# Product 6 of a fused spectral filter and feed-forward kernel: its second half's partial sums in the "kept" buffers, its rows of x in "fs" and "fx", and the loads of the last tile issued during the tile before

## The chip, the cores and the metric

The kernel runs on one core of one Trainium2 chip. The metric is the device time of one execution in microseconds, lower is better. Each core has a TensorE (PE) for matmuls, a VectorE (DVE), a ScalarE (ACT), a GpSimd (POOL) and a SyncE (SP), whose work here is to issue transfers. SyncE and ScalarE each have a queue of transfers of their own, and every engine works through its instructions in the order in which the program gives them.

## The reference

```
x = A_x                                  # 2048 x 1024
xn = layernorm(x)
X = rfft2(xn) * (w_r + 1j * w_i)
s = irfft2(X)                            # 2048 x 1024
h = silu(xn @ w1)                        # 1024 -> 3584
g = silu(h @ w2)                         # 3584 -> 1024
return x + s * g
```

All inputs and the output are float32, with 2048 rows in all.

## The kernel before

The program is one stream of Python that writes the instructions of all engines in an order made by hand. It has three long parts: `xn @ w1` (the matmuls of line 456) with the forward transform beside it, then `h @ w2` (lines 534 to 536) with the filter and the inverse transform beside it, and a short end. Products of float32 numbers are made from three float16 matmuls (high by high, high by low, low by high).

**Seven products instead of eight.** `h @ w2` is computed over groups of 128 rows and halves of 512 columns. Instead of the eight block products of a 2 by 2 block matrix product, seven products of sums and differences of blocks are formed (line 32 names the left factors, line 33 the blocks of w2), and the outputs are put together from them by additions. The products are numbered m = 0 to 6, and each has eight tiles j = 0 to 7: g = j // 4 says which pair of row classes (c = 2g and 2g + 1), p = j % 4 which 128 rows of these. The loop at line 1545 runs over `seq`, all (m, j) with m outermost, so the last eight tiles are those of product 6, and this document calls them tile 0 to tile 7. "First half" is tiles 0 to 3 (g = 0), "second half" tiles 4 to 7.

**One tile.** `mm2` (line 530) does half of a tile's contraction in 21 matmuls of 512 columns (k = 0 and k = 1). The hidden activations `ht` come from memory by `load_h` (line 513), two tiles ahead, on ScalarE's queue. The last tile is cut into three pieces of 256, 128 and 128 columns (line 1552), so that its arithmetic after the matmuls can begin earlier.

**What product 6 does with its result.** It completes two finals per tile. `load_parts` (line 524) reads two partial sums of 128 x 512 back from memory, `pl` from `pd[2, j]` and `pd[0, j]`, on SyncE's queue. When the tile's matmuls are done, `evac` (lines 600 to 602) subtracts the product from the one and adds it to the other on VectorE (lines 601 and 602). `final` (line 620) applies silu on ScalarE (line 622), in place. `finish_out` (line 613) multiplies by the spectral part `s` (line 615) and adds x (line 616) on VectorE, again in place, and puts the store to the output (line 618) on SyncE's queue, or, for the two last pieces of one of the halves, on ScalarE's.

**Rows.** The 128 x 512 pieces of `s` (`fs`) and of x (`fx`) that `finish_out` needs are "rows": `rows_for` (line 540) loads them on SyncE's queue, `ahead_rows` (line 554) calls it early. In the first half of product 6 both are loaded, so a tile has four of them; in the second half `s` is still in its buffer (`resident`, line 1336; the profile calls it `rows`), so only two pieces of x are loaded.

**Stages.** Work after the matmuls is spread over the following tiles by `settle` (line 1421): between the halves of tile j + 1 come first `finish_out` of tile j - 1 and then lines 601 and 602 of tile j; at the end of tile j + 1 come the two activations of tile j. Then `load_parts` and `ahead_rows` of tile j + 1 are written (lines 1568 and 1569), and after them `tick` (line 175) puts out the stores of tile j - 1. So SyncE's queue holds, tile after tile: two partial sums, the rows, two stores of the tile two before. For the last tile `load_parts` and `ahead_rows` stand ahead of its first piece (lines 1550 and 1551).

**Buffers.** `tile_of` (line 203) takes a buffer from a group named by a tag. The buffers of a tag are used in turn: a new user waits until the last reader or writer of that buffer is done. The tags that matter:

| tag | buffers of 128 x 512 | used by |
|---|---|---|
| kept | 8 | running sums of products 0 to 5 (one for each j), then the rows of product 6 |
| pt | 6 | partial sums that are written (products 1, 3, 5) or read back (4, 6) |
| fs | 3 | rows of `s` for finals of other products |
| fx | 2 | rows of x for finals of other products |

A partial sum that is read back is overwritten by lines 601, 602, 622, 615 and 616 and then stored from the same buffer, so its buffer becomes free when that store has landed. A row's buffer is free when VectorE has read it.

Of the kernel before, what the change touches and what calls it, by code (L numbers as in the profile page):

```python
# [10 lines left out]
F32 = mybir.dt.float32  # L11
# [116 lines left out]
def spectral_ffn(ctx, tc, x, w_r, w_i, w1, w2, ca, kc, ci, tw, pm, out):  # L128
# [15 lines left out]
    H = {"p": hstack.enter_context(tc.tile_pool(name="hid", bufs=1))}  # L144
    pf = ctx.enter_context(tc.tile_pool(name="pf", bufs=4, space=PSUM))
    pt = ctx.enter_context(tc.tile_pool(name="pt", bufs=2, space=PSUM))
# [28 lines left out]
    def tick():  # L175
        due = []
        for d in deferred:
            d[0] -= 1
            if d[0] <= 0:
                due.append(d)  # L180
        for d in due:
            deferred.remove(d)
            d[1]()
# [7 lines left out]
    def store(tag, n, fn):  # L191

        d = [n, None]

        def run():
            held[tag].remove(d)
            fn()

        d[1] = run
        held.setdefault(tag, []).append(d)  # L200
        deferred.append(d)

    def tile_of(pool, shape, dtype, name, tag, bufs):
        while len(held.get(tag, ())) >= bufs - 1:
            d = held[tag][0]
            deferred.remove(d)
            d[1]()
        return pool.tile(shape, dtype, name=name, tag=tag, bufs=bufs)
# [302 lines left out]
    part, ht = {}, {}  # L511

    def load_h(m, j, k, queue=nc.scalar):
        t_ = fp.tile([128, 7, 2, 128], F16, name=f"ht{m}_{j}_{k}", tag="w1", bufs=7)
        queue.dma_start(t_, hd[PRODUCTS[m], j // 4][:, j % 4, 7 * k:7 * k + 7])
        ht[m, j, k] = t_
# [4 lines left out]
    rows = {}  # L521
    READS = ((), (), (), (), (1, 0), (), (2, 0))

    def load_parts(m, j):
        for k in READS[m]:
            t_ = tile_of(H["p"], [128, 512], F32, f"pl{m}_{j}_{k}", "pt", 6)
            nc.sync.dma_start(t_, pd[k, j])
            part[k, j] = t_

    def mm2(m, j, ps, k, cols=slice(0, 512)):  # L530
        for q in range(7):
            hh, w = ht[m, j, k][:, q], w2t[m, k][:, q, :, cols]
            first, last = (k + q == 0), (k + q == 7)
            nc.tensor.matmul(ps, hh[:, 0], w[:, 0], start=first, stop=False)  # L534
            nc.tensor.matmul(ps, hh[:, 0], w[:, 1], start=False, stop=False)  # L535
            nc.tensor.matmul(ps, hh[:, 1], w[:, 0], start=False, stop=last)  # L536

    kept = {}

    def rows_for(c, p, h, pool, tags):  # L540

        hsl = slice(h * 512, (h + 1) * 512)
        if (c, p) in sstore:
            sstore.pop((c, p))()
        t_ = []
        for name, src, (tag, bufs) in (("fs", sd[c, p], tags[0]), ("fx", xs[4 * c + p], tags[1])):
            if name == "fs" and (c, p) in resident:
                t_.append(resident[c, p][:, hsl])
                continue
            t_.append(tile_of(pool, [128, 512], F32, f"{name}{c}_{p}_{h}", tag, bufs))  # L550
            nc.sync.dma_start(t_[-1], src[:, hsl])
        return t_

    def ahead_rows(m, j):
        g, p = j // 4, j % 4
        tags = (("kept", 8), ("kept", 8)) if m == 6 else (("fs", 3), ("fx", 2))
        for c, h in FINALS[m]:
            if (2 * g + c, p) in stile and (2 * g + c, p, h) not in rows:
                rows[2 * g + c, p, h] = rows_for(2 * g + c, p, h, H["p"], tags)

    def acc(m, j, ps, cols=slice(0, 512)):
        tt = nc.vector.tensor_tensor
        g, p = j // 4, j % 4
        ahead_rows(m, j)

        def fresh(name):
            return tile_of(H["p"], [128, 512], F32, f"{name}_{j}", "pt", 6)

        def keep(k, t_):
            store("pt", 3, lambda: nc.sync.dma_start(pd[k, j], t_))  # L570

        def evac():
            if m == 0:
                kept[j] = H["p"].tile([128, 512], F32, name=f"kept{j}", tag="kept", bufs=8)
                nc.scalar.activation(kept[j], ps, AF.Copy)
            elif m == 1:
                t_ = fresh("c11")
                tt(t_, kept[j], ps, op=OP.subtract)
                keep(0, t_)
            elif m == 2:  # L580
                tt(kept[j], kept[j], ps, op=OP.add)
            elif m == 3:
                t_ = fresh("c21")
                nc.scalar.activation(t_, ps, AF.Copy)
                tt(kept[j], kept[j], ps, op=OP.subtract)
                keep(1, t_)
            elif m == 4:
                t_, u = part.pop((1, j)), part.pop((0, j))
                tt(t_, t_, ps, op=OP.add)
                tt(u, u, ps, op=OP.add)  # L590
                keep(0, u)
                return final(2 * g + 1, p, 0, t_)
            elif m == 5:
                t_ = fresh("c12")
                nc.scalar.activation(t_, ps, AF.Copy)
                tt(kept[j], kept[j], ps, op=OP.add)
                keep(2, t_)
                return final(2 * g + 1, p, 1, kept.pop(j))
            else:
                t_, u = part[2, j][:, cols], part[0, j][:, cols]  # L600
                tt(t_, t_, ps, op=OP.subtract)  # L601
                tt(u, u, ps, op=OP.add)
                a_, b_ = final(2 * g, p, 1, t_, cols), final(2 * g, p, 0, u, cols)

                def both():
                    x_, y_ = a_(), b_()
                    return (lambda: (x_ and x_(), y_ and y_(), None)[2]) if x_ or y_ else None

                return both

        return evac

    def finish_out(tag, c, p, h, o, s_, x_, cols=slice(0, 512)):
        first = h * 512 + cols.start
        nc.vector.scalar_tensor_tensor(o, s_, s_sc, o, op0=OP.mult, op1=OP.mult)
        nc.vector.tensor_tensor(o, o, x_, op=OP.add)
        queue = nc.scalar if cols.start and h else nc.sync
        store(tag, 1, lambda: queue.dma_start(outs[4 * c + p][:, first:first + cols.stop - cols.start], o))

    def final(c, p, h, o, cols=slice(0, 512)):  # L620
        def act():
            nc.scalar.activation(o, o, AF.Silu, scale=c2)  # L622
            tag = "kept" if h and c % 2 else "pt"
            if (c, p) not in stile:
                store(tag, 1, lambda: nc.sync.dma_start(gd[c, p, h], o))
                fins[c, p, h] = True
                return None
            t_ = rows.get((c, p, h)) or rows_for(c, p, h, H["p"], (("fs", 3), ("fx", 2)))
            return lambda: finish_out(tag, c, p, h, o, *(v[:, cols] for v in t_), cols)

        return act
# [778 lines left out]
    with tc.manual_schedule():  # L1410
# [21 lines left out]
        def after(ev):  # L1432
            settle()
            fresh_ev[0] = ev
            tick()
            work()
# [108 lines left out]
        for n, (m, j) in enumerate(seq):  # L1545
            if 0 < n < len(seq) - 2:
                for k in range(n == 1, 2):
                    load_h(*seq[n + 2], k, nc.scalar)
            if n == len(seq) - 1:
                load_parts(m, j)  # L1550
                ahead_rows(m, j)
                for b, cols in enumerate((slice(0, 256), slice(256, 384), slice(384, 512))):
                    ps = pf.tile([128, cols.stop - cols.start], F32, name=f"pb{m}_{j}_{b}", tag="ff")
                    for k in range(2):
                        mm2(m, j, ps, k, cols)
                    for _ in range(4):
                        settle()
                        tick()
                    after(acc(m, j, ps, cols))
                break  # L1560
            ps = pf.tile([128, 512], F32, name=f"pb{m}_{j}", tag="ff")
            for k in range(2):
                while ready2[0] < m * NP + 7 * k + 6:
                    slot(wq)
                mm2(m, j, ps, k)
                if k == 0:
                    settle()
                    load_parts(m, j)
                    ahead_rows(m, j)
                    tick()  # L1570
                    work()
            if j == 7:
                done2[0] = m + 1
            after(acc(m, j, ps))
            if m == 0:
                slot(wq)
# [38 lines left out]
```

## Time and profile before

| what | value |
|---|---|
| median of 3 runs | 1241.05 us |
| lowest and highest of them | 1239.05 and 1243.32 us |
| the profiled execution, whole | 1238.48 us |
| its span, first to last instruction | 1236.6 us |
| PE busy | 1221.4 us |
| DVE busy | 998.6 us |
| ACT busy | 467.3 us |
| POOL busy | 117.3 us |
| moved by DMA | 293.67 MB, mean 237 GB/s |
| TensorE clock granted, mean | 0.998 |

Times inside the profile are microseconds from the start of the span, unless marked as ns. A row of the timeline gives the start, the length, the engine, the line of the kernel, the operation, the buffer written and those read, the shape, and in brackets the idle time before it with what ended it. Rows of transfers are marked SPq or ACTq for the queue; their length is that of the issue, not of the transfer, and several alike are joined (x2). Buffer numbers are left out in the profile, so all partial sums are `pl`; which tile a row belongs to follows from the order. In the chain of waits each step is followed back to what released it, and a transfer's length there runs from its issue to its landing.

### The profile page before, as it was taken

The page shows a single profiled execution, that of the slowest core. Times are in us where ns is not written, and L with a number is a line of the kernel's source. Part 1 is how long each engine was busy: PE and PEld are TensorE (multiplying, and loading weights), DVE is VectorE, ACT ScalarE, POOL GpSimd, SP SyncE. Part 2 cuts the span into 40 slices and gives each one's busy share as a digit, 9 for nine tenths or more (in the row PEclk, how much of TensorE's full clock was granted, in tenths as well). Part 3 has the DMA queues.
Part 4 walks back from the last instruction along what each step waited for, and adds up shares of the span by engine and source line. Part 5 has one row for each costly group of instructions (what it writes and reads, how often), then busy time and mean ns, then how long its engine had stood idle before and what let it go on. Part 6 is the DMA issues. An engine that isn't in the chain of part 4 may idle for free.

```text
span 1236.6 us, 19106 instructions
## 1 busy us (share of the span) xinstructions
PE 1221.4 (99%) x7033; PEld 624.6 (51%) x7033; DVE 998.6 (81%) x1970; ACT 467.3 (38%) x614; POOL 117.3 (9%) x245
## 2 busy tenths in 40 slices
PE   8999999999999999999999999999999999999997
PEld 5545445444544454445445555554455555555544
DVE  7687988899798898886959899985196678798885
ACT  4865344333454565344533222122032222342212
POOL 2330000001000000010001121114111110000000
PEclk9999999999999999999999999999999999999999
DMA  8487476655768898759899999987979999997677
GB/s 251 136 171 186 134 224 204 186 147 166 218 178 237 283 280 242 213 178 272 206 287 223 281 256 200 303 251 238 294 206 275 293 287 320 319 348 292 223 261 231
DMA packets 271102, 293.67 MB, mean 237 GB/s; under 512 B 40096, under 2 KB 198816, under 8 KB 270624
## 3 DMA queue, kind: packets, MB, share of 16 engines
q1 hardware_dynamic: 250992, 233.66, 65.4%
q10 hardware_dynamic: 15984, 51.45, 12.0%
q0 software_dynamic: 4032, 7.34, 3.4%
q8 instruction: 55, 0.90, 0.3%
q14 instruction: 39, 0.32, 0.1%
HBM read 185.95 MB, written 102.25 MB: 233 GB/s over the span
## 4 chain that ended last, share of the span: by engine, by line
PE 87%; DMA 6%; DVE 4%; ACT 1%; issue 1%; SPq 0%; POOL 0%; ACTq 0%; DVEq 0%; POOLq 0%
PE pa L456 45%; PE pb L534 11%; PE pb L536 11%; PE pb L535 11%; DMA out_dram<-pl 2%; PE fx L945 2%; PE id L1285 1%; DMA sd<-s 1%; PE fx L947 1%; PE iu L1195 1%; PE fx L946 1%; ACT xp L700 1%; PE iu L1203 1%; DMA pl<-pd 1%; DMA fs<-sd 1%
## 5 line engine op out<-in xcount | busy, mean ns | idle before, releaser
L456 PE MATMUL pa<-xnT,w 128*128 128x512 f16 x2688 | 585.2, 379 | 1.1 <-ACT w L251 0.7
L456 PEld LDWEIGHTS <-w 128*128 128x128 f16 x2688 | 261.7, 98 | 312.1 <-DVE w L254 1.3
L534 PE MATMUL pb<-w,ht 128*128 128x512 f16 (+2 forms) x812 | 300.6, 372 | 0.0
L535 PE MATMUL pb<-w,ht 128*128 128x512 f16 (+2 forms) x812 | 300.6, 372 | 0.0
L536 PE MATMUL pb<-w,ht 128*128 128x512 f16 (+2 forms) x812 | 300.6, 372 | 0.0
L536 PEld LDWEIGHTS <-ht 128*128 128x128 f16 x812 | 79.3, 98 | 91.2
L534 PEld LDWEIGHTS <-ht 128*128 128x128 f16 x812 | 79.4, 98 | 86.8
L535 PEld LDWEIGHTS <-ht 128*128 128x128 f16 x812 | 79.3, 98 | 86.8
L465 ACT ACTIVATE h<-pa,s 128x512 f32<-128x512 f32 x112 | 75.5, 678 | 120.9 <-PE pa L456 108.9
L251 ACT ACTIVATE w<-jr,sc 128x512 f16<-128x512 f32 x98 | 68.1, 713 | 78.3 <-DMA jr<-in_B_w_dram 39.4
L254 DVE SCALAR_TENSOR_TENSOR hoone<-h,hs,hoone 128x2048 f16<-128x2048 f32 x28 | 65.7, 2345 | 8.9 <-ACT hoone L251 8.9
L254 DVE SCALAR_TENSOR_TENSOR w<-jr,sc,w 128x512 f16<-128x512 f32 x98 | 71.0, 743 | 2.1 <-ACT w L251 2.1
L251 ACT ACTIVATE hoone<-h,hs 128x2048 f16<-128x2048 f32 x28 | 56.0, 1998 | 38.5 <-DVE h L499 25.1
L251 ACT ACTIVATE hosum<-hr,hs 128x1536 f16<-128x1536 f32 x28 | 44.1, 1574 | 65.2 <-DVE hr L495 31.7
L972 ACT ACTIVATE zq<-Z,zs 128x1024 f16<-128x1024 f32 x16 | 18.4, 1149 | 107.6 <-DVE Z L1046 60.8
L254 DVE SCALAR_TENSOR_TENSOR hosum<-hr,hs,hosum 128x1536 f16<-128x1536 f32 x28 | 50.7, 1812 | 3.8 <-ACT hosum L251 3.8
L494 DVE TENSOR_TENSOR hr<-h 128x1024 f32<-128x1024 f32 x28 | 34.2, 1221 | 23.2 <-ACT h L465 23.1
L251 ACT ACTIVATE w<-w1r,rs 128x1024 f16<-128x1024 f32 x28 | 32.0, 1145 | 46.6 <-DVE w L254 31.4
L274 DVE TENSOR_REDUCE m<-w1r 128x1 f32<-128x1024 f32 x28 | 33.8, 1211 | 17.9 <-DMA w1r<-in_B_w_dram 17.9
L622 ACT ACTIVATE pl<-pl,c 128x512 f32<-128x512 f32 (+2 forms) x28 | 17.6, 657 | 72.3 <-DVE pl L601 33.9
L945 PE MATMUL fx<-vq,kq 128*128 128x256 f16 x192 | 43.2, 273 | 0.0
L946 PE MATMUL fx<-vq,kq 128*128 128x128 f16 x192 | 42.1, 219 | 0.0
(219 smaller groups left out, 1526.2 us busy)
## 6 DMA issues: line engine op xcount, KB each, us to landing
w1r<-in_B_w_dram SPq DMA_DIRECT2D x28, 512.0 KB, 6.3
hd_sum<-hosum SPq DMA_DIRECT2D x56, 256.0 KB, 2.9
hd_one<-hoone SPq DMA_DIRECT2D x56, 256.0 KB, 3.6
hd_dif<-hoone SPq DMA_DIRECT2D x56, 256.0 KB, 3.2
w2m<-in_B_w_dram SPq DMA_DIRECT2D x28, 512.0 KB, 5.2
ht<-hd_dif ACTq DMA_DIRECT2D x32, 448.0 KB, 6.0
jr<-in_B_w_dram SPq DMA_DIRECT2D x56, 256.0 KB, 6.8
ht<-hd_sum ACTq DMA_DIRECT2D x32, 448.0 KB, 5.5
```

The lines of the kernel that those rows point to most:

```text
L251: nc.scalar.activation(hi, raw, AF.Copy, scale=scale)
L254: nc.vector.scalar_tensor_tensor(lo, raw, scale, hi, op0=OP.mult, op1=OP.subtract)
L274: nc.vector.tensor_reduce(m1[:, i:i + 1], raw[i], axis=AX.XY, op=OP.max, apply_absolute_value=True)
L456: nc.tensor.matmul(ps, w[:, wh, d], xt[:, xh, d], start=(n == 0), stop=(n == 23))
L465: nc.scalar.activation(hq[:, 2 * (c % 2) + f % 2], ps, AF.Silu, scale=s1[:, f:f + 1])
L494: tt(sums[:, 0:2], hq[:, 0::2], hq[:, 1::2], op=OP.subtract)
L534: nc.tensor.matmul(ps, hh[:, 0], w[:, 0], start=first, stop=False)
L535: nc.tensor.matmul(ps, hh[:, 0], w[:, 1], start=False, stop=False)
L536: nc.tensor.matmul(ps, hh[:, 1], w[:, 0], start=False, stop=last)
L945: nc.tensor.matmul(o, k[:, c, kh, 1], v[:, c, vh], start=(n == 0), stop=False)
L946: nc.tensor.matmul(ps[:, c, 0], k[:, c, kh, 2], v[:, c, vh, 128:256], start=False, stop=False)
L972: nc.scalar.activation(zqs[q][:, 0, :, 16 * j:16 * j + 16], zs_[u], AF.Copy, scale=zs)
```

## The change

Three edits, all of them around product 6:

- The partial sums of tiles 4 to 7 are read into buffers of tag "kept" (`home`), two for each tile, and those of the first half stay in "pt". The tag is handed on to `final` so that the stores are counted under the right tag.
- The rows of x of tiles 4 to 7 go to other tags: for the half of columns h = 1 to "fs", for h = 0 to "fx", and in tile 7 to "pt".
- `load_parts` and `ahead_rows` of tile 7 are called during tile 6, right after those of tile 6, and no longer ahead of tile 7's first piece. `load_parts` passes over partial sums that have been asked for already.

```diff
+    def home(m, j):
+        return ("kept", 8) if m == 6 and j >= 4 else ("pt", 6)
+
     def load_parts(m, j):
         for k in READS[m]:
-            t_ = tile_of(H["p"], [128, 512], F32, f"pl{m}_{j}_{k}", "pt", 6)
+            if (k, j) in part:
+                continue
+            t_ = tile_of(H["p"], [128, 512], F32, f"pl{m}_{j}_{k}", *home(m, j))
             nc.sync.dma_start(t_, pd[k, j])
             part[k, j] = t_
...
     def ahead_rows(m, j):
         g, p = j // 4, j % 4
-        tags = (("kept", 8), ("kept", 8)) if m == 6 else (("fs", 3), ("fx", 2))
         for c, h in FINALS[m]:
+            tags = (("kept", 8), ("kept", 8)) if m == 6 else (("fs", 3), ("fx", 2))
+            if m == 6 and j >= 4:
+                tags = (("kept", 8), ("fs", 3) if h else ("fx", 2) if j < 7 else ("pt", 6))
             if (2 * g + c, p) in stile and (2 * g + c, p, h) not in rows:
...
-                a_, b_ = final(2 * g, p, 1, t_, cols), final(2 * g, p, 0, u, cols)
+                tag = home(m, j)[0]
+                a_, b_ = final(2 * g, p, 1, t_, cols, tag), final(2 * g, p, 0, u, cols, tag)
...
-    def final(c, p, h, o, cols=slice(0, 512)):
+    def final(c, p, h, o, cols=slice(0, 512), tag=None):
+        tag = tag or ("kept" if h and c % 2 else "pt")
+
         def act():
             nc.scalar.activation(o, o, AF.Silu, scale=c2)
-            tag = "kept" if h and c % 2 else "pt"
...
             if n == len(seq) - 1:
-                load_parts(m, j)
-                ahead_rows(m, j)
                 for b, cols in enumerate((slice(0, 256), slice(256, 384), slice(384, 512))):
...
                     load_parts(m, j)
                     ahead_rows(m, j)
+                    if (m, j) == (6, 6):
+                        load_parts(m, 7)
+                        ahead_rows(m, 7)
                     tick()
                     work()
```

## The prediction

> **What bounds the kernel now.** I read the busy time of each engine by stretches first, then the chain of waits that ended last, then the timeline of SyncE's queue, of TensorE and of VectorE over the last 45 us.
>
> Stretches (length, then PE, PEld, DVE, ACT, POOL busy with their counts, TensorE clock, DMA share, GB/s):
>
> ```profile
> 0.00:93.00 93.00, 87.18 (x472) 47.30 (x473) 69.04 (x102) 59.52 (x53) 25.21 (x62) 1.00 0.71 186
> 93.00:1229.08 1136.08, 1134.24 (x6563) 577.33 (x6561) 925.36 (x1854) 406.38 (x558) 92.07 (x183) 1.00 0.82 242
> 1229.08:1236.60 7.52, 0.00 (x0) 0.00 (x0) 4.21 (x15) 1.39 (x4) 0.00 (x0) 0.71 0.45 155
> ```
>
> TensorE is busy for all but 1.84 us of the middle 1136 and all but 5.82 us of the first 93. Then follow 7.52 us in which it does nothing. An edit that touches only the last product's second half can't shorten TensorE's work; it can only shorten this tail, or starve TensorE before it.
>
> What the tail is made of, by the chain of waits (start, length, what):
>
> ```profile
> 1211.00 5.90 DMA out_dram<-pl
> ...
> 1218.77 5.26 DMA out_dram<-pl
> ...
> 1224.41 4.35 DMA fx<-in_A_x_dram
> 1228.86 0.42 DVE pl L616
> ```
>
> These are transfers, not arithmetic. The queue of SyncE says which:
>
> ```profile
> 1199.90 2.00 SPq L527 DMA_DIRECT2D pl<-pd  x2
> ...
> 1208.59 0.89 SPq L527 DMA_DIRECT2D pl<-pd  x2
> ...
> 1216.30 0.94 SPq L527 DMA_DIRECT2D pl<-pd  x2
> ...
> 1218.30 0.85 SPq L618 DMA_DIRECT2D out_dram<-pl  x2
> 1223.43 0.94 SPq L527 DMA_DIRECT2D pl<-pd  x2
> 1224.41 0.90 SPq L551 DMA_DIRECT2D fx<-in_A_x_dram  x2
> ```
>
> The four pl rows are the partial sums of tiles 4, 5, 6 and 7 of product 6. Six "pt" buffers hold three tiles' pairs, so tile 7 needs the pair of tile 4, and that is free only when tile 4's two stores (issued at 1218.30) have landed: the second took 5.26 us to 1224.03. Tile 7's partial sums are thus asked at 1223.43 and its rows of x at 1224.41, when TensorE is already through the first 256 columns of that tile. SyncE's own waits show the pattern (us in total, times, longest):
>
> ```profile
> SPq L527 <- DMA out_dram<-pl: 17.6, 8, 4.8
> ```
>
> Now the end itself, TensorE beside VectorE (start, us, engine, line):
>
> ```profile
> 1219.42 0.38 PE L536 MATMUL pb<-w,ht 128*128 128x512 f16 x1
> ...
> 1224.12 0.27 PE L536 MATMUL pb<-w,ht 128*128 128x256 f16 x1
> ...
> 1228.86 0.22 PE L536 MATMUL pb<-w,ht 128*128 128x128 f16 x1
> ```
>
> ```profile
> 1219.84 0.69 DVE L601 TENSOR_TENSOR pl<-pl,pb 128x512 f32<-128x512 f32 x1 [1.98 <-PE pb L536]
> ...
> 1223.59 0.69 DVE L616 TENSOR_TENSOR pl<-pl,fx 128x512 f32<-128x512 f32 x1
> 1226.16 0.42 DVE L601 TENSOR_TENSOR pl<-pl,pb 128x256 f32<-128x256 f32 x1 [1.88 <-DMA pl<-pd]
> ...
> 1228.86 0.42 DVE L616 TENSOR_TENSOR pl<-pl,fx 128x256 f32<-128x256 f32 x1 [1.22 <-DMA fx<-in_A_x_dram]
> ...
> 1230.06 0.28 DVE L601 TENSOR_TENSOR pl<-pl,pb 128x128 f32<-128x128 f32 x1
> ...
> 1231.99 0.28 DVE L601 TENSOR_TENSOR pl<-pl,pb 128x128 f32<-128x128 f32 x1
> ```
>
> Tile 6 is taken up 0.04 us after its last matmul ends (1219.42 + 0.38 to 1219.84). The first piece of tile 7 is ready at 1224.39 (1224.12 + 0.27) but taken up at 1226.16, and stops again 1.22 us for x. The two last pieces queue behind it on VectorE: the last starts at 1231.99, though TensorE ended at 1229.08 (1228.86 + 0.22). That is 2.91 us of lateness in the tail, and all of it is transfers that were asked late.
>
> **The change part by part.** *Partial sums of tiles 4 to 7 in "kept".* The eight kept buffers hold, in this order, the rows of finals of tiles 0, 1, 2, 3 (four each, in turn). Tiles 4 and 5 now take the four of tile 2, tiles 6 and 7 the four of tile 3. Those are freed by VectorE's finish (lines 615, 616) and by no store:
>
> ```profile
> 1197.06 0.69 DVE L616 TENSOR_TENSOR pl<-pl,fx 128x512 f32<-128x512 f32 x1
> ...
> 1198.45 0.69 DVE L616 TENSOR_TENSOR pl<-pl,fx 128x512 f32<-128x512 f32 x1
> ...
> 1202.70 0.69 DVE L616 TENSOR_TENSOR pl<-pl,fx 128x512 f32<-128x512 f32 x1
> 1203.31 0.68 DVE L601 TENSOR_TENSOR pl<-pl,pb 128x512 f32<-128x512 f32 x1
> 1206.86 0.69 DVE L602 TENSOR_TENSOR pl<-pl,pb 128x512 f32<-128x512 f32 x1 [2.87 <-DMA pl<-pd]
> ...
> 1210.20 0.69 DVE L616 TENSOR_TENSOR pl<-pl,fx 128x512 f32<-128x512 f32 x1
> ```
>
> The first two rows end tile 2's halves at 1197.75 and 1199.14, the third ends tile 3 at 1203.39. So tile 4's pair, asked at 1199.90 and after, can be asked from 1197.75; tile 5's from 1199.14 in place of 1208.59; tile 6's from 1203.39 in place of 1216.30. Counts of instructions, bytes and the order of TensorE, VectorE and ScalarE stay as they are; the same matmuls are issued. What comes sooner first is the idle 2.87 us ahead of line 602 of tile 4: up to 2.87 us of VectorE, worth 0 at the end, since TensorE runs on over it to 1229.08 and tile 6 already waits 1.98 us for TensorE alone.
>
> *Rows of tiles 4 to 7.* With four kept buffers gone to partial sums, x goes to "fs" (three buffers) and "fx" (two), last used by product 5, and once to "pt". Only x is loaded here; the spectral part of these tiles is resident. First waits: the third user of fx (tile 6) and the fourth of fs (tile 7) need tile 4's finish, 1210.89 today (1210.20 + 0.69). This adds a wait that was not there. Queued behind it on SyncE stand tile 7's loads and tile 4's stores; the stores need the same finish anyway.
>
> *Tile 7 asked at tile 6.* Two partial sums, two rows of x: four issues of 0.33 to 0.5 us each, moved ahead of tile 4's two stores. If tile 4's finish stays at its time now, they leave by about 1213.5 (1210.89 plus five issues of up to 0.5); if it comes 2.87 us sooner, by 1210.6. What a landing takes, over all transfers that read or write pl since 1150, and as a median by kind since 1190:
>
> ```profile
> DMA to landing us min/median/max: 1.5/4.5/7.8
> ...
> pl<-pd SPq DMA_DIRECT2D x10, 256.0 KB, 2.7
> fx<-in_A_x_dram SPq DMA_DIRECT2D x10, 256.0 KB, 5.0
> ```
>
> Best case: 1210.6 + 2.7 = 1213.3; worst: 1213.5 + 7.8 = 1221.3. VectorE wants the partial sums at 1224.43 and x some 1.5 us later, so they are there by 3 us at least. I take the late one; it changes nothing. Tile 4's stores go out up to 2 us later behind these, and nothing waits for their buffers any more. Cost of this part if that cover were gone: each us past 1224.43 is a us at the end.
>
> A shared counter matters too. Transfers wait for others that they have nothing to do with:
>
> ```profile
> SPq L570 <- DMA ht<-hd_sum: 5.9, 1, 5.9
> ...
> 1206.84 0.33 ACTq L515 DMA_DIRECT2D ht<-hd_sum  x1
> ...
> 1207.27 1.33 ACT L622 ACTIVATE pl<-pl,c 128x512 f32<-128x512 f32 x2 [6.16 <-DMA out_dram<-pl]
> ```
>
> A store of product 5 waits for hidden activations because the program hands its DMA semaphores round in turn; the load at 1206.84 on ScalarE's queue, for tile 7, delays the activation of tile 4 in the same way. The new order shifts these pairings. Bounds: a gain of up to 3 us for that activation (line 601 ended at 1203.99, it began at 1207.27), or a wait of one landing, at most 7.8 us, on a load that TensorE wants from 1219.64 on and that leaves by 1206.84 now. Both lie in the 9 us and more ahead of tile 7; I take 0.
>
> *Sum.* First piece: taken up at 1224.39 + 0.04 = 1224.43; VectorE is free at 1224.28 (1223.59 + 0.69). It lasts as now, 1226.16 to 1230.06, less the 1.22 for x: 2.68, to 1227.11. Second piece: 1230.06 to 1231.99, 1.93, to 1229.04. Last piece: not before 1229.08 + 0.04 = 1229.12. From its start to the end of the span 4.61 us pass now (1231.99 to 1236.60) and will again. New span 1233.73, **2.87 us less**. The profiled execution took 1238.48, of which 1.88 lie around its span of 1236.60, so 1235.61. The median shown is 1241.05, 2.57 above it (lowest 1239.05): with the same gain **1238.2 us, 0.23% faster**. Within 0.3%, about what a measurement of this kernel can tell from no change, I call it the same.
>
> A rule that speaks against this: SyncE's row above, 17.6 us of waits of the queue itself, shows loads standing still at the head. The Trainium skill, "DMA: Bandwidth & Descriptors", section "Anatomy of one DMA — SWDGE (gpsimd) path", says that the DMA engines never wait on semaphores; the wait is on the issuing sequencer before dispatch. The trace agrees (longest 4.8 us at line 527). By that rule tile 7's loads are early only as long as tile 4's finish is; by the rows it is, and the sum stays.
>
> **Rivals.**
> (1) *The runs lose more in the tail than the profiled one.* The extra 2.57 us of the median must lie in the head (5.82 us idle), the middle (1.84), the tail (7.52) or outside the span (1.88). The tail has the largest part and is a chain of store, load and arithmetic. If half of the extra is there, the gain is 2.87 + 1.29 = 4.2 us: 1236.9; if all, 5.4: 1235.6. I put it at 1236.2. Against it: the head waits for transfers too.
> (2) *The loads crowd each other.* Peaks in the traffic since 1190 (GB/s in 40 slices) reach 414, the mean of the stretch is 243:
>
> ```profile
> GB/s 68 225 337 346 145 309 377 414 380 214 99 280 333 297 385 292 282 264 265 225 394 169 14 159 312 138 274 384 73 187 340 255 370 401 323 148 116 58 56 0
> DMA packets 6391, 11.40 MB, mean 243 GB/s; under 512 B 716, under 2 KB 1484, under 8 KB 6387
> ```
>
> There is room, but if x for tile 7 still came as late against its piece as now while its partial sums came in time, 1.22 stays and the gain is 1.65 or less: 1239.4 to 1241.
> (3) *Slower.* Place: the wait of tile 6's x at the head of SyncE's queue, in front of tile 7's loads. Should tile 4's finish, or the buffer that x needs, come only with the end of tile 6's finish (1224.28), then that x and four loads leave from there, the first x of tile 7 some 1.7 us later than the 1224.41 of today, and the end moves by it: 1242.8 on the median. It decides from a finish of tile 4 after about 1219; it is at 1210.89 now, held up by the 2.87 us of a load that comes sooner, so I see no cause.
> (4) *It doesn't do what it says*: buffers are handed out otherwise, tile 7's partial sums still wait for a store. 1241.05. The rotation seen in the queue (tile 4 behind tile 1's store, tile 7 behind tile 4's) speaks against it.
>
> **How the numbers follow.** Forecast 0.52, (1) 0.30, (2) 0.10, (3) 0.06, (4) 0.02. The line at 0.3% is 3.7 us; the runs shown lie 2 us to either side of their median, so of the forecast's 0.52 I count 0.17 beyond the line and 0.35 within. (1) gives 0.29 and 0.01; (2) and (4) count as the same, 0.12; (3), half beyond its price by the spread of runs, gives 0.05 slower and 0.01 the same. Together faster 0.46, same 0.49, slower 0.05. The range runs from (1) at its full, 1235.4, over the forecast with the spread of a median, to the better half of (2), 1240.8; outside remain (3), (4) and the rest of (2).
>
> **What would show it.** Right: tile 7's partial sums and x issued on SyncE before 1215 and ahead of tile 4's stores; tile 4's line 602 with no wait for a load; line 601 of the first piece released by TensorE at about 1224.4; the last piece starting within 0.2 us of TensorE's end; from TensorE's end to the span's end 4.65 us in place of 7.52. Wrong: a wait of lines 601, 602 or 616 for a load in tile 7; TensorE ending later than 1229.1; a tail over 6 us; or a tail as forecast while the runs change by something else than 3 us, which would put the difference outside the last tile.

## The result, and the profile after

| | kernel before | changed kernel |
|---|---|---|
| median of 11 runs each | 1243.02 us | 1238.23 us |
| lowest to highest | 1239.05 to 1248.68 | 1234.49 to 1241.62 |
| ratio after / before | | 0.9952, 95% interval 0.9934 to 0.9970 |
| profiled execution, whole | 1238.48 | 1235.84 |
| its span | 1236.6 | 1234.1 |

By the ratio the change made the kernel 0.48% faster, which is 6.0 us (3.7 to 8.2 by its interval); the two medians differ by 4.79 us and the two profiled executions by 2.64. First the stretches of the changed kernel, with the cut where its TensorE ends (columns as before: length, PE, PEld, DVE, ACT, POOL, clock, DMA share, GB/s):

```profile
0.00:93.00 93.00, 86.20 (x472) 46.93 (x473) 69.05 (x102) 59.61 (x53) 25.21 (x62) 1.00 0.71 187
93.00:1229.41 1136.41, 1134.54 (x6563) 578.25 (x6560) 928.24 (x1862) 407.32 (x560) 92.14 (x183) 1.00 0.83 243
1229.41:1234.07 4.66, 0.00 (x0) 0.00 (x0) 1.72 (x7) 0.69 (x2) 0.00 (x0) 0.93 0.21 58
```

The tail fell from 7.52 to 4.66 us. TensorE itself ended 0.33 us later than before, and that is what keeps the span from 1233.73. The later end comes from the head, where TensorE is idle for 6.80 us in place of 5.82, long before product 6.

SyncE's queue in the timeline of the changed kernel, where the lines have moved (532 is the load of partial sums, 556 that of rows, 626 the store):

```profile
1198.39 1.61 SPq L532 DMA_DIRECT2D pl<-pd  x2
...
1203.58 1.73 SPq L532 DMA_DIRECT2D pl<-pd  x2
...
1209.71 1.25 SPq L532 DMA_DIRECT2D pl<-pd  x2
1211.52 0.82 SPq L556 DMA_DIRECT2D fx<-in_A_x_dram  x2
1212.51 0.99 SPq L532 DMA_DIRECT2D pl<-pd  x2
1213.80 0.97 SPq L556 DMA_DIRECT2D fx<-in_A_x_dram  x2
1215.09 16.74 SPq L626 DMA_DIRECT2D out_dram<-pl  x10
```

Tiles 4, 5, 6 and 7 now ask at 1198, 1204, 1210 and 1212.5, where it was 1200, 1209, 1216 and 1223. Tile 7's four loads stand ahead of tile 4's stores, 11 us sooner than before. Then VectorE (608 and 609 were 601 and 602, 624 was 616), and TensorE's last matmul of the first piece and its last of all:

```profile
1203.02 0.69 DVE L624 TENSOR_TENSOR pl<-pl,fx 128x512 f32<-128x512 f32 x1
1204.18 0.69 DVE L608 TENSOR_TENSOR pl<-pl,pb 128x512 f32<-128x512 f32 x1 [0.47 <-DMA pl<-pd]
1204.99 0.69 DVE L609 TENSOR_TENSOR pl<-pl,pb 128x512 f32<-128x512 f32 x1
...
1207.83 0.69 DVE L624 TENSOR_TENSOR pl<-pl,fx 128x512 f32<-128x512 f32 x1
...
1224.76 0.42 DVE L608 TENSOR_TENSOR pl<-pl,pb 128x256 f32<-128x256 f32 x1 [0.24 <-PE pb L541]
...
1227.47 0.28 DVE L608 TENSOR_TENSOR pl<-pl,pb 128x128 f32<-128x128 f32 x1
...
1229.44 0.29 DVE L608 TENSOR_TENSOR pl<-pl,pb 128x128 f32<-128x128 f32 x1
```

```profile
1224.44 0.27 PE L541 MATMUL pb<-w,ht 128*128 128x256 f16 x1
...
1229.19 0.22 PE L541 MATMUL pb<-w,ht 128*128 128x128 f16 x1
```

The first piece is released by TensorE and no longer by a load, 0.05 us behind its last matmul; the last piece starts 0.03 us behind TensorE's end. No row of tile 7 waits for a transfer. VectorE's work on the first two pieces (1224.76 to 1229.44) now takes as long as TensorE needs for the other two, so the last piece finds both engines done at nearly the same time.

### The profile page after: what moved, and what is told of

Read it like the earlier page. It is cut to its first block, busy times and chain, and to the rows that moved or that the text cites. A ratio compares the mean times of both kernels' runs of the same rounds, so it can differ in the third digit from the quotient of the medians.

```text
span 1234.1 us, 19097 instructions
## 1 busy us (share of the span) xinstructions
PE 1220.7 (99%) x7033; PEld 625.2 (51%) x7033; DVE 999.0 (81%) x1970; ACT 467.6 (38%) x614; POOL 117.3 (10%) x245
## 4 chain that ended last, share of the span: by engine, by line
PE 75%; DVE 11%; DMA 9%; issue 2%; ACT 1%; SPq 0%; POOL 0%; DVEq 0%; ACTq 0%; POOLq 0%
PE pa L456 45%; PE pb L539 8%; PE pb L541 8%; PE pb L540 8%; DVE Z L1055 2%; DMA wq<-in_A_w_i_dram 2%; DMA sd<-s 2%; PE id L1294 2%; DMA zd<-zq 1%; DMA ht<-hd_sum_d 1%; DVE T L1020 1%; DVE w L254 1%; PE iu L1204 1%; ACT xp L709 1%; PE iu L1212 1%
## 5 line engine op out<-in xcount | busy, mean ns | idle before, releaser
L274 DVE TENSOR_REDUCE m<-w1r 128x1 f32<-128x1024 f32 x28 | 33.8, 1210 | 16.1 <-DMA w1r<-in_B_w_dram 16.1
```

What stands on the lines that cost most here:

```text
L274: nc.vector.tensor_reduce(m1[:, i:i + 1], raw[i], axis=AX.XY, op=OP.max, apply_absolute_value=True)
```

## The experiments

Theory: the gain is the lateness of tile 7's loads and nothing else, so whatever gets them there before 1224 gives it all. Rivals: the place of the request is needed as well as the buffers; the sooner release for tiles 4 to 6 has a part; ordinary executions gain more than the profiled one.

**e1, the new buffers without the earlier request.**

```diff
+                load_parts(m, j)          # tile 7, ahead of its first piece, as before the change
+                ahead_rows(m, j)
...
-                    if (m, j) == (6, 6):
-                        load_parts(m, 7)
-                        ahead_rows(m, 7)
```

> The new buffers stay, tile 7's loads go back to their old place ahead of tile 7's first piece. Theory 1 (the buffers alone free the loads, the earlier place adds nothing): tile 7's partial sums leave SyncE behind tile 4's stores, at about 1214 to 1218 us and not at 1223, land before 1224, line 608 of the first piece is released by TensorE, the tail from TensorE's end is 4.7 us, ratio as that of the whole change, 0.995. Theory 2 (the earlier place is needed): the first piece still waits for a load, tail 6 to 7.5 us, ratio 0.998 to 1.000.

Measured: ratio 0.9960 (0.9942 to 0.9977), median 1235.63 of 7. SyncE's queue, VectorE at the first piece, and the stretch from TensorE's end on:

```profile
1211.19 0.99 SPq L626 DMA_DIRECT2D out_dram<-pl  x2
1212.48 0.98 SPq L532 DMA_DIRECT2D pl<-pd  x2
1213.75 1.01 SPq L556 DMA_DIRECT2D fx<-in_A_x_dram  x2
```

```profile
1223.72 0.42 DVE L608 TENSOR_TENSOR pl<-pl,pb 128x256 f32<-128x256 f32 x1 [0.24 <-PE pb L541]
```

```profile
1228.37:1233.05 4.68, 0.00 (x1) 0.00 (x0) 1.72 (x7) 0.69 (x2) 0.00 (x0) 0.87 0.20 58
```

Theory 1, and the loads are even sooner than I had expected: 1212.48, though they stand behind two stores. The place in the program is not the time: here SyncE issued them 11 us before the matmuls of the first piece were done. With a tail of 4.68 us against 4.66, the third edit of the change is worth nothing beside the other two.

**e2, new buffers for tile 7 alone** (tiles 4 to 6 as before, tile 7 asked during tile 6).

```diff
-        return ("kept", 8) if m == 6 and j >= 4 else ("pt", 6)
+        return ("kept", 8) if m == 6 and j == 7 else ("pt", 6)
...
-            if m == 6 and j >= 4:
-                tags = (("kept", 8), ("fs", 3) if h else ("fx", 2) if j < 7 else ("pt", 6))
+            if m == 6 and j == 7:
+                tags = (("kept", 8), ("fs", 3) if h else ("fx", 2))
```

> Only tile 7 gets new buffers (partial sums in kept, x in fs and fx) and is loaded during tile 6; tiles 4, 5 and 6 stay in pt and kept as before. Theory 1 (only tile 7's lateness is on the path): tile 4's line 609 keeps its wait of some 2.9 us for a load, tile 7's loads leave at 1217 to 1220 us, the tail is 4.7 us and the ratio 0.995. Theory 2 (the sooner release of tiles 4 to 6 is part of the gain): tail between 5 and 7.5 us, ratio 0.997 or above.

Measured: ratio 0.9966 (0.9947 to 0.9984) and a tail of 5.65 us. The tail lies in the range of theory 2; the ratio decides nothing, since its interval reaches into the range of both. As theory 1 had it, line 609 of tile 4 keeps its wait for a load (3.67 us). SyncE's queue, VectorE, and the stretch from TensorE's end on:

```profile
1218.38 0.94 SPq L532 DMA_DIRECT2D pl<-pd  x2
1219.38 0.90 SPq L556 DMA_DIRECT2D fx<-in_A_x_dram  x2
1220.32 0.90 SPq L532 DMA_DIRECT2D pl<-pd  x2
1221.26 0.91 SPq L556 DMA_DIRECT2D fx<-in_A_x_dram  x2
```

```profile
1225.49 0.69 DVE L624 TENSOR_TENSOR pl<-pl,fx 128x512 f32<-128x512 f32 x1 [0.53 <-DMA fx<-in_A_x_dram]
1226.14 0.42 DVE L608 TENSOR_TENSOR pl<-pl,pb 128x256 f32<-128x256 f32 x1
1226.75 0.42 DVE L609 TENSOR_TENSOR pl<-pl,pb 128x256 f32<-128x256 f32 x1 [0.19 <-DMA pl<-pd]
```

```profile
1229.75:1235.40 5.65, 0.00 (x1) 0.00 (x0) 2.65 (x10) 0.80 (x3) 0.00 (x0) 0.84 0.56 193
```

Tile 6's loads (the first row) still wait for tile 3's stores; tile 7's have their buffers but stand behind them. Eight loads go out within 3.8 us, and tile 6's x is so late that VectorE is still finishing tile 6 when the first piece is ready (about 1225.05, 4.70 us ahead of TensorE's end as in the changed kernel), and takes it up at 1226.14. So the theory falls in its narrow form: the release of tiles before tile 7 is part of the gain.

**e8, new buffers for tiles 6 and 7.** Run after the others, to see whether it is tile 6, and not tiles 4 and 5 or the shared semaphores.

```diff
-        return ("kept", 8) if m == 6 and j == 7 else ("pt", 6)
+        return ("kept", 8) if m == 6 and j >= 6 else ("pt", 6)
...
-            if m == 6 and j == 7:
+            if m == 6 and j >= 6:
```

> As e2, but tile 6 too has its partial sums in kept and its x in fs and fx; tiles 4 and 5 stay as before. Theory 1 (e2 kept a tail of 5.6 us because tile 6's loads still waited for tile 3's stores and stood in the queue ahead of tile 7's): tile 6's loads leave before 1216, tile 7's before 1219, line 608 of tile 7's first piece is released by TensorE, tail 4.7 us. Theory 2 (e2's tail came from shared semaphores or from tiles 4 and 5): a wait for a load stays in the first piece, tail 5.2 us or more.

Measured: ratio 0.9971 (0.9953 to 0.9989), and the whole tail is back, in an execution whose TensorE ended at 1230.81. SyncE's queue, VectorE, and the stretch:

```profile
1215.01 1.64 SPq L532 DMA_DIRECT2D pl<-pd  x2
...
1217.91 0.95 SPq L532 DMA_DIRECT2D pl<-pd  x2
```

```profile
1226.15 0.42 DVE L608 TENSOR_TENSOR pl<-pl,pb 128x256 f32<-128x256 f32 x1 [0.24 <-PE pb L541]
```

```profile
1230.81:1235.48 4.67, 0.00 (x0) 0.00 (x0) 1.72 (x7) 0.69 (x2) 0.00 (x0) 0.95 0.21 58
```

Tile 6's loads leave 3.4 us sooner than in e2, in an execution that is 1.1 us later, and that is enough; tile 7's two rows of x left at 1219.10 and after, a little later than the 1219 that I had written. That is theory 1: it is tile 6, and tiles 4 and 5 in the old buffers cost nothing at the end of this trace.

**e5, everything new but asked late.** Tile 7's loads behind its first piece's matmuls.

```diff
                     for _ in range(4):
                         settle()
                         tick()
+                    load_parts(m, j)
+                    ahead_rows(m, j)
                     after(acc(m, j, ps, cols))
```

> All new buffers, but tile 7's partial sums and x are asked only behind its first piece's matmuls, so that SyncE issues them behind the stores of tiles 5 and 6. Theory 1 (when the loads leave is all that counts, not which buffers they use): the partial sums leave at about 1225, land at 1228, x lands at about 1230; the first piece waits for both, the tail is 8 to 9.5 us, longer than the 6.9 and 7.5 of the kernel before; ratio 0.999 to 1.003. Theory 2 (the tail shrank through the buffers themselves, for instance through the stores that are out of the way): tail 4.7 to 6 us, ratio 0.996.

Measured: ratio 1.0000 (0.9981 to 1.0020), median 1242.90. The traced execution ended its matmuls late, at 1237.37; against that end the loads leave 4.5 us ahead, as expected. SyncE's queue and the stretch:

```profile
1231.11 1.72 SPq L626 DMA_DIRECT2D out_dram<-pl  x2
1232.88 0.92 SPq L532 DMA_DIRECT2D pl<-pd  x2
1233.84 0.90 SPq L556 DMA_DIRECT2D fx<-in_A_x_dram  x2
```

```profile
1237.37:1246.71 9.34, 0.00 (x0) 0.00 (x0) 5.46 (x18) 2.40 (x6) 0.00 (x0) 0.74 0.20 61
```

Theory 1: with the same buffers as the changed kernel the tail is 9.34 us, and the whole gain is gone. When the loads leave is what counts. The late end of the matmuls in this execution has another cause, which the last section shows.

**e3, e4, e6, e7, e9, e10: the two kernels again, unchanged.** The ratio was twice what the trace had shown. Copies of both kernels, timed beside each other, show how far their times and their tails spread.

> The changed kernel once more, for a second trace and for the spread. Theory 1 (the gain is the tail, and its size differs from execution to execution with the transfers): tail 4.7 us again, spans differ by 3 us or more because of idle TensorE time elsewhere, at the head. Theory 2 (the tail of the changed kernel is itself longer in some executions): a tail above 5.5 us in this trace or a span that grows with it. Ratio 0.993 to 0.998.

> The kernel before once more, for a second trace and for the spread of spans. Theory 1 (ordinary executions of the kernel before lose more in the tail than the first profiled one): tail from TensorE's end 8.5 to 11 us, TensorE's end within 1 us of 1229, first piece of tile 7 waiting over 3 us for its loads. Theory 2 (they lose it elsewhere): tail 7.5 us, TensorE's end 2 us or more later. Ratio 0.999 to 1.001.

> The changed kernel again, timed in one job with a copy of the kernel before, so that copy stands against copy. Theory 1 (the change is worth its tail, 2.2 to 2.9 us, and what the first comparison showed beyond that is the granted TensorE clock of the single executions): its median lies 2 to 3 us under that of e7, and executions at one granted clock differ by the same. Theory 2 (ordinary executions gain 4 to 6 us): median 4 us or more under that of e7. Tail 4.7 us in its trace by both.

> A copy of the kernel before. Theory 1: ratio to the kernel before 0.998 to 1.001, and where it differs from 1 the granted clocks of the two sets of executions differ too, about 1.2 us for each 0.001. Theory 2: ratio 0.9995 to 1.0005 and clocks alike. Tail 6.9 to 7.6 us in its trace by theory 1, 8.5 us or more by theory 2.

> One more trace of the kernel before, for the spread of its tail, which was 7.5, 6.9 and 9.6 us so far. Theory 1 (the lateness of tile 7's loads hangs on the transfers of each execution): a tail between 6.5 and 10 us, and the later tile 7's second partial sum lands after the first piece's matmuls, the longer. Theory 2 (the tail follows TensorE's end alone): 7 us whenever TensorE ends at 1229.

> As e9, a further trace: by theory 1 a tail between 6.5 and 10 us in step with the landing of tile 7's x, by theory 2 7 us whenever TensorE ends at 1229.

| | median us | ratio (interval) | tail in its trace |
|---|---|---|---|
| e3, after | 1237.81 of 12 | 0.9965 (0.9950 to 0.9980) | 4.66 |
| e6, after | 1237.47 of 12 | 0.9952 (0.9933 to 0.9970) | 4.65 |
| e4, before | 1239.87 of 12 | 0.9992 (0.9977 to 1.0007) | 6.89 |
| e7, before | 1240.73 of 12 | 0.9982 (0.9966 to 0.9998) | 9.62 |
| e9, before | one run, 1240.91 | | 8.90 |
| e10, before | one run, 1239.26 | | 8.63 |
| the kernel before, beside e1 to e4 | 1242.02 of 30 | | |
| the same, beside e5 to e7 | 1243.20 of 29 | | |
| the same, beside e8 to e10 | 1241.45 of 17 | | |

The longest of these tails, the stretch from TensorE's end and VectorE at the first piece of e7:

```profile
1231.78:1241.40 9.62, 0.00 (x1) 0.00 (x0) 5.25 (x17) 1.89 (x5) 0.00 (x0) 0.72 0.58 206
```

```profile
1230.79 0.42 DVE L601 TENSOR_TENSOR pl<-pl,pb 128x256 f32<-128x256 f32 x1 [1.84 <-DMA pl<-pd]
1232.80 0.42 DVE L602 TENSOR_TENSOR pl<-pl,pb 128x256 f32<-128x256 f32 x1 [1.59 <-DMA pl<-pd]
```

In the execution of the prediction the second partial sum cost 0.17 us after the first; here 1.59. The tail of the kernel before is thus 7.52, 6.89, 9.62, 8.90 and 8.63 us in five executions, 8.31 in the mean, while that of the changed kernel is 4.66, 4.66 and 4.65. It doesn't follow TensorE's end: e4 and e10 end their matmuls within 0.2 us of each other, at 1229.04 and 1228.86, with tails of 6.89 and 8.63, which speaks against theory 2 of e9 and e10.

What it follows is how long before TensorE's end tile 7's partial sums are asked for. In e4 and in e7:

```profile
1222.46 0.96 SPq L527 DMA_DIRECT2D pl<-pd  x2
```

```profile
1228.09 1.41 SPq L527 DMA_DIRECT2D pl<-pd  x2
```

That is 6.58 us ahead of the end in e4 and 3.69 in e7; it is 5.65 in the execution of the prediction, 4.74 in e10 and 4.05 in e9. In the order of these leads the tails are 6.89 (e4), 7.52, 8.63 (e10), 8.90 (e9) and 9.62 us (e7): the later the request, the longer the tail, without an exception. This is theory 1 of e9 and e10. Where a program with other buffers asks late, as in e5 (4.49 us ahead), the tail is 9.34 us, some 0.6 us above this row.

The other expectations fared as follows. e4's tail fits neither of its theories, 8.5 to 11 us or a later end of TensorE; the longer tails that its theory 1 wanted are in e7, e9 and e10. For e7 theory 1 said a tail of 6.9 to 7.6 us and missed, while its ratio is within what theory 1 said. e3 has the tail that its theory 1 expected, but the spans of the changed kernel (1234.07, 1235.94 and 1232.96 us) don't differ by idle time at the head: the longest, e3, has 5.72 us of it, the execution profiled first 6.80.

Copy against copy the medians differ by 2.06 (e3 and e4) and 3.26 us (e6 and e7). Theory 1 of e6 wanted 2 to 3 us and theory 2 4 or more; 3.26 lies between, nearer to theory 1. With 12 runs of each, such a difference is uncertain by about 2 us. All 24 against 24 differ by 2.7 us in the mean (1.5 to 3.9, a 95% interval from resampling the runs). The executions of the kernel before that the ratios are taken against, the same program as e4 and e7, are slower than these copies: by the ratios 1.0 us in e4, where the interval holds 1, and 2.2 us in e7, where it does not. So part of the 6.0 us is probably no gain of the change, and the ratios of e1, e2 and e8 lean the same way.

## Why the prediction was right, and where its size was off

*The time and the direction.* 1238.2 was forecast and 1238.23 measured, but the agreement is partly luck: the median before came out as 1243.02 and no longer as 1241.05, so the gain came out larger than the 2.87 us, 4.79 by the medians and 6.0 by the ratio. The call of "the same", within 0.3%, did not hold: the interval of the ratio, 0.9934 to 0.9970, lies on the faster side of that line. Faster had been given 0.46, the same 0.49.

*The signs.* All that was to show the prediction right is in the rows above. Two signs of being wrong came up as well. TensorE ended at 1229.41 and not by 1229.1, because of the head. And the tail came out as forecast while the runs changed by more than 3 us. That was to put the difference outside the last tile; the copies show that some of it is in the last tile of other executions.

*The sum, term by term, in the traced execution.* First piece taken up 0.05 us behind its matmuls (0.04 forecast), 2.71 us long (1224.76 to 1227.47; 2.68), second 1.97 (1.93), third 0.03 behind TensorE's end (0.04), from there to the end of the span 4.63 (4.61). The tail is 4.66 against 4.65. The step that used the row of x's wait as a thing to take off was right.

*Buffers.* Tile 4's pair leaves at 1198.39; tile 5's was expected from 1199.14 and left at 1203.58, tile 6's from 1203.39 and left at 1209.71. I had looked only at the release of the buffer and not at what stands ahead in the queue, nor at waits for other transfers. SyncE's own waits in the changed kernel from 1192 on (us in total, times, longest) show loads of partial sums (line 532) that wait for loads of hidden activations and of rows of s, which their own buffers don't need:

```profile
SPq L532 <- DMA fs<-sd: 2.4, 1, 2.4
...
SPq L532 <- DMA ht<-hd_sum: 1.6, 2, 1.1
```

It cost nothing, since TensorE covers it. Tile 7's loads had left by 1214.8 against the 1213.5 at worst that I allowed, 9.9 us before its first piece was ready.

*The 2.87 us ahead of line 602.* Gone, as said (line 609 of tile 4 at 1204.99, no wait), and worth 0.

*The activation of tile 4* bounded by a gain of 3 us: with line 608 ended at 1204.87, it began

```profile
1204.90 1.54 ACT L632 ACTIVATE pl<-pl,c 128x512 f32<-128x512 f32 x2 [3.48 <-DVE pl L608]
```

and not at 1207.27. Worth 0 at the end, as taken.

*The size: the step that failed* is "with the same gain", which carried the tail of one execution over to the runs. The tail fell by 2.86 us in the pair of executions profiled first, as forecast, but by 8.31 - 4.66 = 3.65 us in the mean over five traces, and by 2.2 to 5.0 in the single ones. That is rival (1) in its mechanism: the chain of store, load and arithmetic runs later in other executions. But of the 2.57 us by which the median lay above the profiled run, the tail holds only 0.79 in the mean (8.31 - 7.52). What makes the executions that the ratios are taken against slower than copies of the same program stays open. Their granted clock is a little lower in the mean (0.9966 over 59, 0.9974 over the 24 copies), which would be about 1 us. It can't be set apart as a cause, though: the mean takes in the tail, where the clock was 0.71 before and 0.93 after the change, so a longer tail lowers it too.

*Rivals (2), (3) and (4)* are refuted by the rows above: no wait of tile 7 for a load, no late finish of tile 4 (1207.83 + 0.69 in place of 1210.89), new buffers taken in the order that was read from the queue. The third edit, which the prediction weighed at length, has no effect next to the first two (e1); its wait for tile 4's finish was over at 1208.52, before SyncE came to it.

## What to carry to other kernels

At the end of a kernel bound by TensorE, look at what releases the first VectorE instruction behind the last matmuls: if it is a load, trace that load back to the buffer that it waits for. Here a buffer that is freed by a store came free a landing later (5.26 us in the execution of the prediction) than one that VectorE frees. The group of buffers was the thing to change: the earlier place of the request added nothing to it (e1), though a place behind the stores undid it (e5). Free the tiles ahead in the same queue too, or their loads hold up the last one (e2). And read such a chain in several executions before giving its size: one kernel's tail lay between 6.9 and 9.6 us.

## What the runs showed of the hardware that I had not expected

The same load of the same program is asked for at 3.69 to 6.58 us before TensorE's end, and the tail grows from 6.89 to 9.62 us with it (the five traces above). Part of it is the landing of like transfers: the second store of tile 4, from issue to landing in the chain of waits, took 4.65 us in e4 and 5.37 in e7.

A TensorE that stands still for a few us can lose more than these. Here are 15 us around the start of the last inverse transform, in e5, where it was idle 3.68 us, and in e6, whose program is the same up to there, where it was idle 1.50:

```profile
1060.00:1075.00 15.00, 11.32 (x84) 6.34 (x82) 6.85 (x14) 3.68 (x7) 0.00 (x0) 0.89 0.91 301
```

```profile
1060.00:1075.00 15.00, 13.50 (x99) 7.45 (x98) 13.04 (x27) 5.19 (x11) 0.00 (x0) 1.00 0.81 269
```

The mean granted clock is 0.89 in the one and 1.00 in the other. In e5 31 matmuls of 512 columns fall into these 15 us and in e6 51; at 0.216 us from one to the next at full clock, 20 matmuls are 4.3 us, for 2.18 us more of idle time. The Trainium skill, "TensorE: Matmul & The Clock Gate", section "Part 1: The HAM clock gate", says that the clock goes to half after an idle window of about 3.4 us. The trace agrees here: after one idle time of 3.68 us the clock was 0.57 from 1071 to 1075.

But the clock fell without such an idle time too. At 843 us stand 18 matmuls of only 8 or 24 columns (lines 1085 to 1087). The 4 us behind them, in e3 and in the execution of the changed kernel that was profiled first, the same program:

```profile
846.00:850.00 4.00, 4.00 (x13) 1.44 (x11) 3.84 (x5) 2.02 (x4) 3.23 (x8) 0.57 0.76 231
```

```profile
846.00:850.00 4.00, 4.00 (x21) 1.78 (x19) 3.78 (x5) 1.96 (x4) 3.29 (x8) 1.00 0.76 242
```

From 843 to 846 TensorE was idle for 0.28 us in e3 and for 0.15 in the other, and yet e3 ran at a clock of 0.57 and did 8 matmuls fewer. In e5, with 0.87 us idle there, the clock was 0.50 from 846 to 852. Why it fell in these and not in the other is not shown. With the wait above, this is about what makes e5's matmuls end 8 us late: 0.87 us idle here, 2.2 us more idle there, and about 5 us by the granted clock, an estimate from these rows. Both places lie outside the change, and e3 shows that the clock is part of why one program's executions differ.
